# Two interleaved attention blocks with gradients: which engine turns the weights, and when

## The chip, the cores and the metric

The kernel runs on one core of a Trainium2 chip. The metric is the device time of one execution in microseconds (us); lower is better.

## The reference

Four residual layers, A, B, A, B, on x of 2048 tokens by 640 features in bf16, with 32 heads of 20. A and B have one set of weights each, used twice.

```python
def A(x):   # linear attention, no mask
    q, k, v = split(layernorm(x) @ A_wqkv)
    pq, pk = phi(q), phi(k)                   # where(t > 0, t + 1, exp(t)) + 1e-6
    o = (pq @ (pk.T @ v)) / (pq . sum(pk))    # per head
    return o @ A_wo
def B(x):   # sliding window of 256, causal
    q, k, v = split(layernorm(x) @ B_wqkv)
    return softmax(mask(q @ k.T / sqrt(20))) @ v @ B_wo
x = x + A(x); x = x + B(x); x = x + A(x); x = x + B(x)
```

The outputs are x and the gradients of grad_out by x, A_wqkv, A_wo, B_wqkv and B_wo. The backward pass multiplies by transposed weights, so four weights are needed turned: Wqkv (640x1920) and Wo (640x640) of A and of B. Turning them is what the change is about.

## The kernel before, in words

Tokens are worked on in 16 tiles of 128 (`TT`). The time has these stages: the **opening** (`a_first`, L940: layer norm and q, k, v of the first A layer, tile by tile, to about 112 us), the sums over all tokens (`a_kv`, L569), the **first pass** (`ab_pass(0)`, L961: the rest of layer A, the whole B layer and the q, k, v of the next A layer, one tile after the other, to about 430 us), again `a_kv`, the **second pass** (`ab_pass(2)`, to about 715 us), and then the backward phases, which the change doesn't touch.

`forward` (L332) doesn't issue instructions directly. Each helper records an operation (`Sched.op`, L94) with its engine, an estimated duration, what it reads and writes, and a due time; `Sched.order` (L126) then plays the engines forward with these estimates and fixes the order of each engine's queue. Every queue is worked off in that order: an instruction that waits holds all behind it on its engine. SyncE (SP) issues most DMAs, ScalarE (ACT) the rest. An operation marked `filler` on TensorE is taken when nothing else is ready for `IDLE` (L23, 300 ns of the estimates). `Ring` is a set of buffers used in turn; a new use waits until the last one is done.

Two ways of turning 128-column blocks are in use. `flip` (L417) is a transposing DMA on SyncE's queue. `turn` (L449) lets TensorE multiply by the identity into PSUM (L462) and ScalarE or VectorE copy the result to SBUF (L465, L467). In the first pass each tile needs such flips of its own: oTA, oTB, QT, KT, hnTB, pqT.

The turned weights are made before as follows, each in pieces of 160 KB that go through SBUF to DRAM (`W`) and are read in the backward phases:

- `wflips` (L906): A's Wqkv (15 pieces) and A's Wo (5), flipped from their copies in SBUF (`Wqkv_A`, and `slabR`, the memory that Wo_A lies in) into the ring pp, then stored. They are spread over the tiles of the first pass (L1031, with `wf` and `ws` in `AT`).
- `bflips` (L919): B's Wqkv (15 pieces), flipped from the input in DRAM into the rings KT, QT and e, then stored, after the first pass (L1048).
- `early_dO` (L712): B's Wo (5 pieces), flipped from SBUF into `WoTB` (in the memory of vv), at the start of the second pass, after `a_kv` is done with vv (`after_kv`).

Other names that matter: hn, the normalised tile, has a single buffer (`hnA`, L371); it is written by VectorE (L480), stored by SyncE (L484) and turned by TensorE. ee, the buffer of exp(q) or exp(k), has four. `s3` and `s1` are the PSUM banks of the attention scores (L821), `singles` the same five banks one by one. `late_q` (L540) recomputes q for six tiles as filler work between the passes.

Of the kernel before, what the change touches and what calls it, by code (L numbers as in the profile page):

```python
# [16 lines left out]
P = 128  # L17
# [69 lines left out]
class Sched:  # L87
# [38 lines left out]
    def order(self):  # L126
        engs = ("PE", "DVE", "ACT", "POOL", "SP")
        for o in self.ops:
            o.after -= o.deps | {o}
            o.nwait = len(o.deps) + len(o.after)  # L130
            for d in o.deps | o.after:
                assert d.idx < o.idx
                d.users.append(o)
        last = {}
        for o in self.ops:
            for b in o.bufs:
                last[b] = o.idx
# [12 lines left out]
        while len(out) < len(self.ops):  # L150
            best = None
            for e in engs:
                if not ready[e]:
                    continue
                t, cands = free[e], ready[e]
                if e == "PE" and self.ahead is not None:
                    cands = [o for o in cands if o.filler or o.rank < front + self.ahead]
                    if not cands:
                        continue
                o = min(cands, key=lambda o: (max(o.est, t) + IDLE * o.filler, o.prio))  # L160
                c = (max(o.est, t), o.prio)
                if best is None or c < best[0]:
                    best = (c, o)
            (t, _), o = best
            e = o.eng
            ready[e].remove(o)
            if o.dma:
                kind, size = o.dma
                if kind == "T":
                    free[e] = t + 1100 + size / 1000  # L170
                    chan = max(chan, t + 800) + size / 140
                else:
                    free[e] = t + (330 if e == "SP" else 200)
                    chan = max(chan, t) + size / 300
                o.end = chan + 2000
            else:
                free[e] = t + o.dur
                o.end = free[e] + (170 if e == "PE" else 0)
            o.start = t
            out.append(o)  # L180
            while front < len(seq) and seq[front].start is not None:
                front += 1
            for u in o.users:
                if o in u.deps:
                    u.est = max(u.est, o.end + (60 if u.eng != e or o.dma else -170 if e == "PE" else 0))
# [15 lines left out]
class Kern:  # L201
# [130 lines left out]
    def forward(self, slabs):  # L332
# [5 lines left out]
        with ExitStack() as st:  # L338
# [78 lines left out]
            def flip(out, in_, size, r, w, **kw):  # L417
                op("SP", 60, lambda: nc.sync.dma_start_transpose(out=out(), in_=in_()), r, w, dma=("T", size), **kw)
# [4 lines left out]
            def av(n):  # L423
                return 170 + 0.834 * n
# [283 lines left out]
            def after_kv(o):  # L708
                o.deps.update(kv_users)
                o.deps.discard(o)  # L710

            def early_dO():  # L712
                for et in range(DT):
                    flip(lambda et=et: WoTB[:, :, et * P:(et + 1) * P], lambda et=et: wsb["Wo_B"][:, et, :], 160 * KB,
                         ["Wo_B", ("rs", 3, 0)], [("WoTB", et)])
                    after_kv(S.ops[-1])
                dma("SP", lambda: W["WoTB"].rearrange("p (a b) -> p a b", a=DT), lambda: WoTB, 800 * KB,
                    [("WoTB", et) for et in range(DT)], [])
                for t in dslabs:
                    op("DVE", 100 + DP * 0.45, lambda t=t: nc.vector.memset(t, 0.0), [], ["dzero"])  # L720
                    after_kv(S.ops[-1])
# [181 lines left out]
                v = src.rearrange("(kt p) n -> p kt n", p=P)  # L903
                dma(eng, lambda: wsb[name][:, k:k + 1, :], lambda: v[:, k:k + 1, :], 2 * P * wsb[name].shape[-1], after, [name])

            def wflips(i, gate):  # L906
                def f():
                    et, part = divmod(i, 4)
                    key, dst, n, a = ("Wqkv_A", "WqTA", self.QTT, part * DT) if part < 3 else ("Wo_A", "WoTA", DT, 0)
                    c0 = part * D if part < 3 else 0  # L910
                    b = R["pp"].buf()
                    keys = [("Wqkv_A", i) for i in range(6)] if part < 3 else [key]
                    view = lambda: b.t.rearrange("p (k q) -> p k q", k=DT)
                    flip(view, lambda: wsb[key][:, et, c0:c0 + D], 160 * KB, keys + [gate], [b])
                    dma("SP", lambda: W[dst].rearrange("p (a b) -> p a b", a=n)[:, a:a + DT, et * P:(et + 1) * P],
                        view, 160 * KB, [b], [])
                return f

            def bflips(i, gate):  # L919
                def f():  # L920
                    et, part = divmod(i, 3)
                    kind = ("KT", "QT", "KT", "e", "e")[i % 5]
                    b = R[kind].buf()
                    view = lambda: (b.t[:, 0:DT, :] if kind != "e" else
                                    b.t.rearrange("p h i q -> p (h i) q")[:, 0:DT, :])
                    flip(view, lambda: self.B_wqkv[et * P:(et + 1) * P, part * D:(part + 1) * D], 160 * KB, [gate], [b])
                    dma("SP", lambda: W["WqTB"].rearrange("p (a b) -> p a b", a=self.QTT)[
                        :, part * DT:(part + 1) * DT, et * P:(et + 1) * P], view, 160 * KB, [b], [])
                return f

            wA = self.A_wqkv.rearrange("(kt p) n -> p kt n", p=P)
            for c0, c1 in ((0, 2), (2, 6)):
# [7 lines left out]
            def a_first(items, l, base, lag=0.0, late=()):  # L940


                for tt in range(TT):
# [14 lines left out]
            AT = {0: dict(wf=-2.296, ws=0.65, num=-2.458, out=-1.707, outb=1.792, step=0.144, qkv=-0.99, wide=0.745, lag=0.42, af=2.042, al=-0.11),  # L958
                  2: dict(lq=-3.207, num=-2.403, out=-1.76, outb=1.696, step=0.086, qkv=-0.985, wide=0.584, lag=0.35, gT=0.745, dO=1.691, dOs=0.137)}

            def ab_pass(l, last):  # L961
# [59 lines left out]
                if last:  # L1021
                    for tt in range(EARLY, TT):
                        items.append((tt + a["lq"], len(items), lambda tt=tt: late_q(l, tt, "mm")))
                    items.append((0.01, len(items), early_dO))
                    spread(items, 15.0, 16.25, [dWo_most(u) for u in range(NA)])
                    for tt in range(TT):
                        for at, f in zip((a["gT"] - 0.5, a["gT"], a["dO"], a["dO"] + a["dOs"]), dO_steps(tt)):
                            items.append((tt + at, len(items), f))
                else:
                    a_first(items, l + 2, a["af"], a["al"], range(TT))  # L1030
                    for i in range(4 * DT):  # L1031
                        t = min(int(a["wf"] + a["ws"] * i), TT - 1)
                        items.append((t + 0.05, len(items), wflips(i, ("rs", 1, t))))
                run(items)

            items = []
# [4 lines left out]
            for i, (k, src) in enumerate((("Wo_A", self.A_wo), ("Wqkv_B", self.B_wqkv), ("Wo_B", self.B_wo))):  # L1041
                for j in range(DT):
                    tt = 1 + 3 * i + j
                    items.append((tt + 0.9, len(items), lambda k=k, src=src, j=j, tt=tt: load_w(k, src, "SP", j, [("vv", tt, 5)])))
            run(items)
            a_kv(0)
            ab_pass(0, False)
            for i in range(3 * DT):  # L1048
                bflips(i, ("rs", 1, TT - 1))()
            for tt in range(EARLY):  # L1050
                late_q(2, tt, filler=True)
            a_kv(2)
            kv_users = {o for t in range(TT) for k in [("pk", t, 2), ("pk", t, 3), ("vv", t, 4), ("vv", t, 5)]
                        for o in S.rd.get(k, ())}
            a_users = {o for i in range(6) for o in S.rd.get(("Wqkv_A", i), ())}
            ab_pass(2, True)
            over = [o for k in ("Wqkv_B", "Wo_A") for o in S.rd.get(k, ())]
# [810 lines left out]
```

## Time and profile before

| | |
|---|---|
| median of three runs | 2163.03 us (2159.4 to 2163.52) |
| the profiled execution | 2163.08 us, span 2161.4 us |
| TensorE busy | 2008.5 us, 93% of the span |
| weight loads (PEld) | 1384.3 us, 64% |
| VectorE busy | 1441.9 us, 67% |
| ScalarE busy | 1191.9 us, 55% |
| GpSimd busy | 879.2 us, 41% |
| SyncE's DMA queue (q1) | 302.44 MB, 72.5% of 16 DMA engines' time |
| ScalarE's DMA queue (q10) | 72.94 MB, 10.9% |

How to read it: the page cuts the span into 40 slices and gives each engine's busy share in tenths, the TensorE clock that was granted (PEclk, in tenths of full speed) and the share of the DMA engines. Rows of a stretch give busy time and, in brackets, the number of instructions. A row of the timeline gives start, duration, engine (SPq and ACTq are DMA issues), line, operation and what was written from what; in square brackets stands the idle time before it and the releaser that the profile infers. "To landing" is the time from the issue of a DMA to its completion.

### The profile page before, as it was taken

To read this page: it belongs to the slowest core of one execution; us is meant where nothing else is said; L and a number is where in the kernel's file an instruction comes from. 1 tells how busy PE (TensorE), PEld (TensorE's weight loads), DVE (VectorE), ACT (ScalarE), POOL (GpSimd) and SP (SyncE) were. 2 spreads that over 40 slices of the span, in tenths; PEclk is the share of its full clock that TensorE was granted. 3 is DMA by queue.
4 is the path that set the end of the run, shared out by engine and by line. 5 is a ranking of instruction groups with operands and counts; after the bars stand their busy time and mean duration, and the time that the engine had idled before them with its cause. 6 is when DMAs were issued, how large, how long until landed. Compare 5 with 4: busy or idle time off the path is not lost. (4 is left out here: it accounts for less than half of the span.)

```text
span 2161.4 us, 67833 instructions
## 1 busy us (share of the span) xinstructions
PE 2008.5 (93%) x27808; PEld 1384.3 (64%) x27808; DVE 1441.9 (67%) x2954; ACT 1191.9 (55%) x1975; POOL 879.2 (41%) x1850
## 2 busy tenths in 40 slices
PE   6878899879999899999899999998999999999999
PEld 4645666556666567777666667655777765666764
DVE  7656677567777489999734459605999984444651
ACT  4617778617888589899522223215889882121430
POOL 1015566506777556666323213203656651221210
PEclk9979999999999989999999999998999989999999
DMA  7449998788999688988997899836998997989843
GB/s 274 171 136 194 191 199 185 173 220 182 211 210 199 144 157 157 159 155 151 200 187 168 208 196 214 181 95 143 154 159 151 166 169 162 195 181 230 186 112 102
DMA packets 964808, 379.70 MB, mean 176 GB/s; under 512 B 844817, under 2 KB 944785, under 8 KB 964241
## 3 DMA queue, kind: packets, MB, share of 16 engines
q1 hardware_dynamic: 887296, 302.44, 72.5%
q10 hardware_dynamic: 77200, 72.94, 10.9%
q8 instruction: 217, 3.56, 0.7%
q14 instruction: 95, 0.77, 0.1%
HBM read 109.02 MB, written 112.07 MB: 102 GB/s over the span
## 5 line engine op out<-in xcount | busy, mean ns | idle before, releaser
L1668 DVE TENSOR_TENSOR ds_sb<-pair,e_sb 128x768 bf16<-128x768 f32 x480 | 438.0, 952 | 58.4 <-PE pair L1629 50.9
L1648 ACT ACTIVATE e_sb<-pair 128x768 bf16<-128x768 f32 x480 | 391.0, 815 | 95.6 <-PE pair L1629 66.3
L841 POOL TENSOR_SCALAR_AFFINE_SELECT e_sb<-e_sb 128x384 bf16<-128x384 bf16 (+1 forms) x512 | 198.2, 406 | 373.7 <-ACT e_sb L832 347.3
L832 ACT ACTIVATE e_sb<-s_ps 128x1152 bf16<-128x1152 f32 (+2 forms) x256 | 273.9, 1070 | 107.0 <-PE s_ps L828 71.0
L1660 POOL TENSOR_SCALAR_AFFINE_SELECT e_sb<-e_sb 128x256 bf16<-128x256 bf16 x448 | 182.1, 407 | 226.9 <-ACT e_sb L1648 226.8
L1302 POOL TENSOR_TENSOR gw<-w,gcar 128x640 f32<-128x640 f32 x64 | 89.4, 1398 | 423.9 <-ACT w L1299 400.4
L1113 PEld LDWEIGHTS <-slabR 128*128 128x128 bf16 x1920 | 185.7, 98 | 116.2 <-DMA slabR<-o 5.8
L1657 POOL TENSOR_SCALAR_AFFINE_SELECT e_sb<-e_sb 128x256 bf16<-128x256 bf16 x512 | 206.5, 406 | 90.1 <-ACT e_sb L1648 90.1
L1693 PEld LDWEIGHTS <-dsT 128*128 128x128 bf16 x2880 | 146.3, 97 | 96.7 <-issue 90.4
L1684 ACT COPY dsT<-dsT_ps 128x768 bf16<-128x768 bf16 x240 | 191.2, 797 | 10.2 <-PE dsT_ps L1681 7.3
L446 PE MATMUL mm_ps<-slabR,hnTB 128*128 128x320 bf16 x960 | 170.5, 309 | 8.4 <-DVE gcar L518 6.1
L1681 PE MATMUL dsT_ps<-ident,ds_sb 128*128 128x128 bf16 x1848 | 158.4, 223 | 1.6 <-ACT dsT L1684 1.1
L1697 PEld LDWEIGHTS <-e_sb 128*128 128x128 bf16 x2880 | 145.2, 96 | 0.0
L1697 PEld LDWEIGHTS <-ds_sb 128*128 128x128 bf16 x2880 | 145.1, 96 | 0.0
L846 POOL TENSOR_SCALAR_AFFINE_SELECT e_sb<-e_sb 128x512 bf16<-128x512 bf16 x224 | 142.5, 636 | 0.0
L835 ACT ACTIVATE e_sb<-s_ps 128x384 bf16<-128x384 f32 (+2 forms) x256 | 119.8, 468 | 36.6 <-PE s_ps L828 10.1
L1113 PE MATMUL dw_ps<-dqkv,slabR 128*128 128x480 bf16 x640 | 134.6, 366 | 0.0
L1113 PE MATMUL dw_ps<-dqkv,om 128*128 128x480 bf16 x640 | 134.2, 366 | 0.0
L1284 ACT ACTIVATE dh<-mm_ps 128x320 f32<-128x320 f32 x64 | 28.0, 437 | 191.6 <-PE mm_ps L1113 153.3
L1629 PE MATMUL pair<-slabR 32*128 32x384 bf16 (+2 forms) x1024 | 121.6, 329 | 11.5 <-DVE ds_sb L1668 5.0
L866 PE MATMUL pv_ps<-v_slab,e_sb 128*128 128x32 bf16 x2880 | 117.7, 177 | 12.9 <-POOL e_sb L846 10.7
L866 PEld LDWEIGHTS <-e_sb 128*128 128x128 bf16 x2880 | 106.0, 96 | 35.6 <-POOL e_sb L846 14.6
(227 smaller groups left out, 4299.3 us busy)
## 6 DMA issues: line engine op xcount, KB each, us to landing
qkvp<-qk_slab SPq DMA_DIRECT2D x64, 256.0 KB, 3.4
hn<-slabR SPq DMA_DIRECT2D x64, 160.0 KB, 3.0
qkvp<-v_slab SPq DMA_DIRECT2D x32, 256.0 KB, 3.5
slabR<-qkvp SPq DMA_DIRECT2D x16, 512.0 KB, 5.2
o<-o SPq DMA_DIRECT2D x48, 160.0 KB, 2.8
eq<-ee ACTq DMA_DIRECT2D x32, 160.0 KB, 3.0
pq<-pp ACTq DMA_DIRECT2D x32, 160.0 KB, 2.0
ek<-ee ACTq DMA_DIRECT2D x32, 160.0 KB, 2.3
```

The lines of the kernel that those rows point to most:

```text
L446: nc.tensor.matmul(ps.t[:, w0:w0 + width], lhsT=lhsT(), rhs=rhs(), start=start, stop=stop)
L832: op("ACT", av(3 * nkt * P), lambda: nc.scalar.activation(e.t[:, 0:3, 0:nkt, :], s3.t[:, :, 0:nkt * P].rearrange("p h (i q) -> p h i q", q=P),
L841: nc.gpsimd.affine_select(out=v, in_=v, compare_op=ALU.is_ge, fill=0.0, base=0, pattern=[[0, h1 - h0], [1, P]], channel_multiplier=-1)
L866: nc.tensor.matmul(pv.t[:, h % 16, :], lhsT=e.t[:, hh, j, :], rhs=vts[j].t[:, h, :], start=(j == 0), stop=(j == nkt - 1))
L1113: nc.tensor.matmul(ps.t[:, w0:w0 + width], lhsT=lhsT(), rhs=rhs(), start=start, stop=stop)
L1648: nc.scalar.activation(E[n][:, 2 * p:2 * p + 2], PR[h][:, :, 0:3 * P].rearrange("p i (j q) -> p i j q", q=P), ACT.Exp, scale=self.c_att)
L1657: nc.gpsimd.affine_select(out=e[:, :, j, :], in_=e[:, :, j, :], compare_op=ALU.is_ge, fill=0.0, base=0, pattern=[[0, 2], [-1, P]], channel ...
L1660: nc.gpsimd.affine_select(out=e[:, :, j, :], in_=e[:, :, j, :], compare_op=ALU.is_ge, fill=0.0, base=-1, pattern=[[0, 2], [1, P]], channel ...
L1668: nc.vector.tensor_mul(DS[n][:, hs], PR.pop(h)[:, :, 0:3 * P].rearrange("p i (j q) -> p i j q", q=P), E[n][:, hs])
L1681: nc.tensor.transpose(ps[:, i, j, :], DS[n][:, 2 * p + i, j, :], self.ident)
L1684: (nc.scalar.copy if by == "A" else nc.vector.tensor_copy)(TSB[h], TPS.pop(h))
L1697: nc.tensor.matmul(a[:, 1 + x, hh, :], lhsT=src[n][:, hh, j, :], rhs=ld[g][rhs][:, q, cs], start=(i == 0), stop=(i == len(dkv) - 1))
```

## The change

The four weights change places and means. A's Wo and **B's Wqkv** are flipped by DMA from the inputs in DRAM during the opening, two pieces per tile from 4.5 tiles on, through the rings KT and e. **A's Wqkv and B's Wo** are turned by TensorE between the passes: each piece is five transposes into one of the three banks of s3, a ScalarE copy of 128x640 into KT or e (or right into `WoTB`), and for A's Wqkv a store of whole rows. These operations are fillers; they wait for the last scores of the first pass, and the first scores of the second pass wait for them all (the line with `items[-1].ops.extend(turned)`), the copies into `WoTB` also for the end of `a_kv`. The planner gets a fixed cost for the new DMAs (kind "B"). The flips of `wflips`, `bflips` and `early_dO` go.

```diff
             if o.dma:
                 kind, size = o.dma
-                if kind == "T":
+                if kind == "B":
+                    free[e], chan_ = t + 1300, t + 2500
+                elif kind == "T":
...
-                o.end = chan + 2000
+                o.end = (chan_ if kind == "B" else chan) + 2000
...
             def early_dO():
-                for et in range(DT):
-                    flip(lambda et=et: WoTB[:, :, et * P:(et + 1) * P], lambda et=et: wsb["Wo_B"][:, et, :], 160 * KB,
-                         ["Wo_B", ("rs", 3, 0)], [("WoTB", et)])
-                    after_kv(S.ops[-1])
...
-            def wflips(i, gate):
...
-            def bflips(i, gate):
...
+            def turn_w(name, n, keys, dst, done, after=()):
+                F = dict(filler=True)
+                for q in range(n):
+                    ps = R["sb"].buf()
+                    ps.make = lambda ps=ps: singles[ps.idx % 3].bitcast(BF).rearrange("p (k q) -> p k q", q=P)
+                    def f(ps=ps, q=q):
+                        for et in range(DT):
+                            nc.tensor.transpose(ps.t[:, et, :], wsb[name][:, et, q * P:(q + 1) * P], self.ident)
+                    o = op("PE", pe([P] * DT), f, keys, [ps], **F)
+                    o.deps.update(o_ for o_ in R["s3"].items[-1].ops if not o_.filler)
+                    turned.append(o)
+                    out, key = dst(q)
+                    turned.append(op("ACT", av(D), lambda ps=ps, out=out: nc.scalar.copy(out(), ps.t[:, 0:DT, :]), [ps],
+                                     [key], **F))
+                    turned[-1].deps.update(after)
...
+                    done(q, out, key)
+            def flip_w(i, gate):
+                def f():
+                    et, part = divmod(i, 4)
+                    src, name, n, a = ((self.B_wqkv, "WqTB", self.QTT, part * DT) if part < 3 else (self.A_wo, "WoTA", DT, 0))
+                    c0 = part * D if part < 3 else 0
+                    kind = ("KT", "e")[i % 2]
+                    b = R[kind].buf()
...
+                    flip(view, lambda: src[et * P:(et + 1) * P, c0:c0 + D], 160 * KB, [gate], [b])
+                    S.ops[-1].dma = ("B", 0)
+                    dma("SP", lambda: W[name].rearrange("p (a b) -> p a b", a=n)[:, a:a + DT, et * P:(et + 1) * P],
+                        view, 160 * KB, [b], [])
...
+            R["sb"] = Ring(3, tiles=singles[0:3], name="sb")
+            def staged(W_, n):
+                def dst(q):
+                    kind = ("KT", "e")[len(turned) // 2 % 2]
...
+                def done(q, out, b):
+                    dma("SP", lambda: W[W_].rearrange("p (a b) -> p a b", a=n)[:, q, :].rearrange("p (k q) -> p k q", q=P),
+                        out, 160 * KB, [b], [])
...
+            for i in range(4 * DT):
+                at = 4.5 + 0.5 * i
+                items.append((at, len(items), flip_w(i, ("rs", 0, int(at) - 1))))
             run(items)
             a_kv(0)
             ab_pass(0, False)
-            for i in range(3 * DT):
-                bflips(i, ("rs", 1, TT - 1))()
             for tt in range(EARLY):
                 late_q(2, tt, filler=True)
             a_kv(2)
...
+            turn_w("Wqkv_A", self.QTT, [("Wqkv_A", i) for i in range(6)], *staged("WqTA", self.QTT))
+            turn_w("Wo_B", DT, ["Wo_B"], lambda q: (lambda: WoTB[:, q, :].rearrange("p (k q) -> p k q", q=P), ("WoTB", q)),
+                   lambda q, out, key: None, kv_users)
+            R["s3"].items[-1].ops.extend(turned)
```

More of the change, by code (lines that the diff above doesn't have):

```diff
@@ L904, in load_w @@
                 dma(eng, lambda: wsb[name][:, k:k + 1, :], lambda: v[:, k:k + 1, :], 2 * P * wsb[name].shape[-1], after, [name])
-            def wflips(i, gate):
+            def turn_w(name, n, keys, dst, done, after=()):
[13 more added lines that the diff above has]
+                    turned[-1].deps.update(after)
+                    turned[-1].deps.discard(turned[-1])
+                    done(q, out, key)
@@ L907, in f @@
+            def flip_w(i, gate):
                 def f():
                     et, part = divmod(i, 4)
-                    key, dst, n, a = ("Wqkv_A", "WqTA", self.QTT, part * DT) if part < 3 else ("Wo_A", "WoTA", DT, 0)
+                    src, name, n, a = ((self.B_wqkv, "WqTB", self.QTT, part * DT) if part < 3 else (self.A_wo, "WoTA", DT, 0))
                     c0 = part * D if part < 3 else 0
-                    b = R["pp"].buf()
-                    keys = [("Wqkv_A", i) for i in range(6)] if part < 3 else [key]
@@ L913, in f @@
-                    view = lambda: b.t.rearrange("p (k q) -> p k q", k=DT)
-                    flip(view, lambda: wsb[key][:, et, c0:c0 + D], 160 * KB, keys + [gate], [b])
-                    dma("SP", lambda: W[dst].rearrange("p (a b) -> p a b", a=n)[:, a:a + DT, et * P:(et + 1) * P],
+                    kind = ("KT", "e")[i % 2]
+                    b = R[kind].buf()
+                    view = lambda: (b.t if kind == "KT" else b.t.rearrange("p h i q -> p (h i) q"))[:, 0:DT, :]
+                    flip(view, lambda: src[et * P:(et + 1) * P, c0:c0 + D], 160 * KB, [gate], [b])
@@ L916, in f @@
+                    S.ops[-1].dma = ("B", 0)
+                    dma("SP", lambda: W[name].rearrange("p (a b) -> p a b", a=n)[:, a:a + DT, et * P:(et + 1) * P],
                         view, 160 * KB, [b], [])
+                    S.ops[-1].dma = ("B", 0)
                 return f
-            def bflips(i, gate):
-                def f():
-                    et, part = divmod(i, 3)
-                    kind = ("KT", "QT", "KT", "e", "e")[i % 5]
-                    b = R[kind].buf()
[L924 to L929, printed above, removed]
+            turned = []
@@ new lines, in forward @@
+            R["sb"] = Ring(3, tiles=singles[0:3], name="sb")
+            def staged(W_, n):
+                def dst(q):
+                    kind = ("KT", "e")[len(turned) // 2 % 2]
+                    b = R[kind].buf()
+                    return (lambda: b.t[:, 0:DT, :] if kind == "KT" else
+                            b.t.rearrange("p h i q -> p (h i) q")[:, 0:DT, :]), b
+                def done(q, out, b):
+                    dma("SP", lambda: W[W_].rearrange("p (a b) -> p a b", a=n)[:, q, :].rearrange("p (k q) -> p k q", q=P),
+                        out, 160 * KB, [b], [])
+                return dst, done
@@ L957, in forward @@
             EARLY = 6
-            AT = {0: dict(wf=-2.296, ws=0.65, num=-2.458, out=-1.707, outb=1.792, step=0.144, qkv=-0.99, wide=0.745, lag=0.42, af=2.042, al=-0.11),
+            AT = {0: dict(num=-2.458, out=-1.707, outb=1.792, step=0.144, qkv=-0.99, wide=0.745, lag=0.42, af=2.042, al=-0.11),
                   2: dict(lq=-3.207, num=-2.403, out=-1.76, outb=1.696, step=0.086, qkv=-0.985, wide=0.584, lag=0.35, gT=0.745, dO=1.691, dOs=0.137)}
@@ L1030, in ab_pass @@
                     a_first(items, l + 2, a["af"], a["al"], range(TT))
-                    for i in range(4 * DT):
-                        t = min(int(a["wf"] + a["ws"] * i), TT - 1)
-                        items.append((t + 0.05, len(items), wflips(i, ("rs", 1, t))))
                 run(items)
```

## The prediction

> **What bounds the kernel now.** I read the page's table of slices first, then the busy times by stage, then by tile, then SyncE's own queue.
>
> ```profile
> PE   6878899879999899999899999998999999999999
> PEclk9979999999999989999999999998999989999999
> DMA  7449998788999688988997899836998997989843
> ```
>
> A slice is 54 us. TensorE has nine tenths almost everywhere from slice 10 on, so the end of the program is set by TensorE's work plus TensorE's gaps. The gaps that this change can touch lie in slices 0 to 8, the forward passes; the built instruction lists of both kernels are the same behind the first tiles of the second pass, so I price nothing after some 520 us. By stage (columns: stretch, length, busy us of PE, PEld, DVE, ACT, POOL, granted clock, DMA share, GB/s):
>
> ```profile
> 45.06:106.91 61.85, 54.34 (x494) 39.57 (x493) 44.27 (x128) 38.96 (x93) 0.00 (x0) 1.00 0.48 170
> 177.64:309.27 131.63, 115.90 (x1885) 79.95 (x1884) 88.84 (x218) 93.73 (x153) 75.72 (x166) 0.94 0.94 191
> 309.27:391.45 82.18, 78.03 (x1352) 55.26 (x1352) 62.85 (x157) 66.87 (x111) 54.87 (x120) 1.00 0.87 190
> 420.00:452.24 32.24, 26.33 (x320) 19.28 (x317) 16.76 (x48) 5.95 (x14) 2.24 (x6) 0.85 0.92 206
> 452.24:480.20 27.96, 20.66 (x183) 13.39 (x182) 22.04 (x56) 4.06 (x11) 0.00 (x0) 1.00 0.95 236
> ```
>
> The reader is to see three things: the opening (first row) uses half of the DMA engines; the first pass has a worse half (second row) and a better one (third); between the passes (last rows) TensorE idles for 13 us and ScalarE has 10 us of work in 60. The first pass by tile, cut where SyncE issues the flip of that tile's pqT:
>
> ```profile
> 193.90:213.00 19.10, 15.08 (x242) 10.42 (x240) 11.14 (x27) 13.01 (x21) 10.48 (x23) 0.86 1.03 203
> 213.00:231.95 18.95, 18.42 (x291) 12.61 (x290) 13.53 (x34) 13.51 (x24) 10.86 (x24) 0.96 0.92 194
> 231.95:252.19 20.24, 15.26 (x257) 10.65 (x257) 12.76 (x31) 13.49 (x22) 10.95 (x24) 0.91 0.87 181
> 291.31:309.27 17.96, 17.02 (x286) 12.05 (x285) 13.26 (x34) 13.53 (x24) 11.05 (x24) 1.00 0.87 195
> 326.14:342.62 16.48, 15.73 (x273) 11.10 (x273) 12.89 (x33) 13.41 (x23) 10.95 (x24) 1.00 0.86 193
> 342.62:359.12 16.50, 15.75 (x273) 11.13 (x273) 12.54 (x33) 13.30 (x23) 11.01 (x24) 1.00 0.88 193
> ```
>
> The same tile takes 19 to 20 us while weight flips stand in SyncE's queue, and 16.5 us as soon as they are over (the last WoTA store is issued at 305.12). Why, the queue shows:
>
> ```profile
> 191.90 1.27 SPq L418 DMA_TRANSPOSE pp<-slabR  x1
> 193.22 0.58 SPq L414 DMA_DIRECT2D WqTA<-pp  x1
> 193.90 1.41 SPq L418 DMA_TRANSPOSE pqT<-slabR  x1
> 195.35 0.66 SPq L414 DMA_DIRECT2D hn<-slabR  x1
> 196.11 1.23 SPq L418 DMA_TRANSPOSE QT<-qk_slab  x1
> ```
>
> A weight flip (pp) and a weight store stand ahead of flips that TensorE needs. QT, issued at 196.11, lands by the QT group's median of 4.2 us at 200.3, and TensorE's next scores wait:
>
> ```profile
> 199.77 0.35 PE L828 MATMUL s_ps<-QT,KT 32*128 32x128 bf16 x12 [2.27 <-ACT e_sb L832]
> ```
>
> The releaser named there is inferred. Such gaps are followed by slices with a lower granted clock: 10 us windows at 0.83 behind this gap, at 0.73 behind one of 2.99 us at 248.40, and none between 300 and 410 us, where gaps stay below 1.4 us.
>
> A second link runs through ScalarE. In the built instruction lists each DMA of SyncE and ScalarE takes one of eight counters in turn and waits for the last DMA on it. So a late flip also holds a ScalarE store, and the arithmetic queued behind it: ScalarE's waits name the flips of pp with 4.7 + 1.2 us up to 305 us, and 5.8 us at 439.67 behind an hn store.
>
> **The change part by part.** The sum is made against the profiled execution, 2163.1 us with a span of 2161.4; the median of the three runs shown is 2163.03, so both are the same place.
>
> Removed from the first pass: 20 flips (1.24 us of issue each) and 20 stores (0.38 to 0.58 us). Eight intervals from 177.64 to 326.14 last 148.5 us; at the later pace of 16.49 they would last 131.9. **Gain 16.6.** What is late next is TensorE itself, 15.7 of 16.5 us. Bounds: of the 16.6, some 7 us is clock, each interval's TensorE time by what its clock lacks (15.08 x 0.14, 18.42 x 0.04, 15.26 x 0.09, 18.68 x 0.08, 16.50 x 0.09); if the dips do not come from the gaps, 9.4 is left. Six of the flips stand ahead of 177 us, in the ramp 106.9 to 177.6. Its largest gaps (2.67 us at 127, 2.26 at 155) end with the normalisation L480, a VectorE chain: I take a gain of 1, from 0 to 3.
>
> Added to the opening: 20 flips from the inputs and 20 stores, two pairs per tile from tile 3 to 13, between the hn stores in SyncE's queue. The pace now is 5.30 us per tile (hn stores from 45.06 to 98.07, ten tiles). Three prices bear on it. (1) Issue: 0.33 + 2 x 1.25 + 2 x 0.5 = 3.8 us per tile, below 5.3. (2) DMA engines: from 420 to 446 us queue q1 carried 12 flips, 12 such stores and 2 hn in 20.3 us of all 16 engines (78.3% of 16, 77.5% of 10), less 0.9 for hn, so 1.6 us a pair; 0.48 x 5.3 + 1.8 x 1.6 = 5.4 us per tile, just full. (3) Landing: hn has one buffer, so each L480 (0.44 us) waits for the store of the tile before. That store lands in 1.9 us here, 2.6 to 3.0 where the DMA share is 0.9; with the one L480 wait of 0.67 us at 49.15 the loop is already near the pace at places. I take 0.6 us for each of ten tiles: **cost 6**. Bounds: 0, if all stays below 5.3; 22, the slow rival below.
>
> [...]
>
> Between the passes: 15 flips of B's Wqkv with stores (400 to 446 us) and 5 of Wo (453 to 466) go. In their place come 20 groups of five TensorE transposes, 20 ScalarE copies of 128x640 and 15 stores of whole rows. On TensorE a group costs 0.28 us from start to start (97.11 to 97.39), 20 of them 5.6 us, of which I hide half in the gaps of 420 to 480 us: +3. The copies, 20 x 0.69 = 13.9 us, fit into ScalarE's 50 idle us; three banks let TensorE run three groups ahead. But the first scores of the second pass now stand behind the last two Wo groups and their copies, 0.2 + 2 x 0.69: +1.6. Against this:
>
> ```profile
> 440.96 2.83 PE L446 MATMUL mm_ps<-Wqkv_A,pqT 128*128 128x320 bf16 x10 [3.36 <-DVE gcar L518]
> ```
>
> This gap is ScalarE held by a store's counter behind an hn store that lands 3.1 us after issue, while q1 is full of flips. Without them I take 2.7 of 3.36, and 1.9 us of slow clock behind it (ten matmuls in 2.83 us, usually 1.58; five at 445.05 in 1.49, usually 0.84). **Net 0**: 3 + 1.6 - 2.7 - 1.9; bounds -5 (all the added work in gaps) and +7 (none in gaps, nothing won back). The 5 Wo flips ahead of the qkvp stores cost nothing now: the gap of 2.67 us at 472 ends with L480 again.
>
> [...]
>
> Sum: -16.6 - 1 + 6 + 0 = -11.6, **2151.5 us**.
>
> **Rivals.**
> 1. The clock of the first pass dips by itself. For: the dips lie in slices that are also full of work. Against: none in 300 to 410 us. 2163.1 - 9.4 - 1 + 6 = **2158.7**.
> 2. The opening hides all: SyncE and DMA have room on average. -16.6 - 1 + 1 + 0: **2146.5**; with the gaps between the passes won too (-5), 2141.5.
> 3. Slower: the eight counters set the opening's pace. A tile then issues 6 + 3.6 = 9.6 DMAs, so each waits for one issued some 4.4 us before; flips land in 3.7 us at the median and 6.0 at most. With 6.0 throughout, 9.6 / 8 x 6.0 = 7.2 us per tile, 1.9 over, and eleven tiles cost +21; with +3 between the passes, 2163.1 - 17.6 + 21 + 3 = **2169.5**. It decides from 6.9 us per tile (5.3 + 17.6 / 11). Against: landing in the first pass, at a DMA share of 1.03, has its median near 3.6.
> 4. The flips were not what slowed the first pass; it gains nothing: -1 + 6, **2168**. Against: the pace changes with the last flip.
>
> **How the numbers follow.** Forecast 0.56, rival 2 0.17, rival 1 0.12, rival 3 0.11, rival 4 0.04. The range, 2141 to 2165, takes in the first three and leaves out the slow ends. A measurement here tells 0.2% (4.3 us) from no change: faster 0.78 (the forecast, rival 2 and part of rival 1), same 0.09, slower 0.13.
>
> **What would show it.** In the profile after: tiles of the first pass near 16.5 us from the start, at clock 1.00; an opening with a pace of 5.9 us, and waits of L480 for hn or of ScalarE for the flips into KT and e_sb; no gap of 3 us near the end of the first pass; one of 1 to 2 us at the first scores of the second. The prediction is wrong if the first pass keeps 19 us tiles, or if the opening's pace is above 6.9.

## The result and the profile after

| | before | after |
|---|---|---|
| median (range) of six runs each | 2162.74 us (2148.88 to 2164.93) | 2144.49 us (2139.10 to 2146.05) |
| profiled execution, span | 2163.08, 2161.4 us | 2145.22, 2143.5 us |

The ratio is 0.9924, with a 95% interval of 0.9903 to 0.9944: faster by 18 us. The page's slices after. Against before, TensorE rises from 8 to 9 in slices 3 and 4, and the DMA engines are fuller in slices 0 and 1, where the flips went (7 and 4 before, 9 and 9 now), and emptier in slice 7 (7 before, 4 now), where flips went away. The clock of the first pass (slices 4 to 7) reads 9 in both, so slices of 54 us are too coarse to show its dips:

```profile
PE   6879999889999899999899999999999999999999
PEclk9989999999999899999899999999999999999999
DMA  9928989469998788987987899847999998989943
```

To compare stages I cut both traces at five events: ScalarE's first store of oA (end of the opening and its sums), the first, ninth and last flip of pqT of the first pass, and the first store of the output x in the second pass. The opening of before from its sixth to its sixteenth store of hn, then three stretches of before (stretch, length, busy us of PE, PEld, DVE, ACT, POOL, clock, DMA share, GB/s):

```profile
45.06:98.07 53.01, 45.72 (x413) 33.21 (x412) 38.29 (x111) 32.91 (x81) 0.00 (x0) 1.00 0.48 171
120.50:177.64 57.14, 45.98 (x490) 28.83 (x490) 35.67 (x85) 19.02 (x46) 14.87 (x38) 0.81 0.66 152
177.64:326.14 148.50, 131.76 (x2158) 91.37 (x2157) 101.48 (x250) 107.04 (x175) 86.73 (x190) 0.94 0.93 191
407.96:506.40 98.44, 77.22 (x926) 51.92 (x923) 62.23 (x161) 32.91 (x74) 20.77 (x50) 0.93 0.80 191
```

The same stretches after:

```profile
50.15:109.62 59.47, 50.96 (x467) 37.32 (x466) 43.03 (x122) 35.66 (x88) 0.00 (x0) 1.00 0.96 250
123.70:178.72 55.02, 45.03 (x484) 28.40 (x484) 35.41 (x85) 18.76 (x46) 13.93 (x36) 0.81 0.39 109
178.72:310.74 132.02, 124.98 (x2167) 87.64 (x2164) 98.56 (x251) 107.25 (x176) 87.75 (x192) 1.00 0.89 189
392.24:490.80 98.56, 82.96 (x1035) 58.92 (x1033) 62.30 (x161) 46.95 (x96) 21.51 (x52) 0.91 0.56 165
```

The eight intervals of the first pass lost 16.5 us: 6.8 are TensorE's busy time (the clock went from 0.94 to 1.00) and 9.7 are gaps (16.7 us idle before, 7.0 after). The ramp ahead of it (from the end of the opening to the first pqT flip) is 2.0 us shorter. The opening's DMA share went from 0.48 to 0.96, and its end came 3.1 us later (120.54, then 123.65). Between the passes the length hardly moved, though TensorE has 5.7 us more work there.

By tile, the first two of the eight intervals now last 13.5 and 18.4 us and the others 16.5 to 17.2. Here are the third and the fourth, and then SyncE's queue. Before, a weight flip and a weight store were issued just ahead of pqT; now the queue is free there, from the end of oTA's issue at 189.1 us until pqT at 192.17:

```profile
210.54:227.03 16.49, 15.79 (x273) 11.34 (x273) 12.84 (x33) 13.64 (x23) 10.95 (x24) 1.00 0.87 193
227.03:243.50 16.47, 15.73 (x273) 11.10 (x273) 12.88 (x33) 13.52 (x23) 10.92 (x24) 1.00 0.92 194
```

```profile
187.88 1.24 SPq L420 DMA_TRANSPOSE oTA<-oA  x1
192.17 1.20 SPq L420 DMA_TRANSPOSE pqT<-slabR  x1
193.43 0.57 SPq L416 DMA_DIRECT2D hn<-slabR  x1
194.09 1.22 SPq L420 DMA_TRANSPOSE oTB<-oB  x1
195.40 1.58 SPq L420 DMA_TRANSPOSE QT<-qk_slab  x1
```

The gap of 3.36 us near the end of the first pass is now 0.24, its ten matmuls take 1.52 us instead of 2.83, and the first scores of the second pass wait for a copy of Wo (TensorE's timeline):

```profile
422.69 1.52 PE L448 MATMUL mm_ps<-Wqkv_A,pqT 128*128 128x320 bf16 x10 [0.24 <-DVE gcar L520]
...
454.56 0.24 PE L826 MATMUL s_ps<-QT,KT 32*128 32x128 bf16 x4 [1.38 <-ACT vv L918]
```

### The profile page after: what moved, and what is told of

Same layout as the page of the kernel before. It is cut to its first block, busy times and chain, and to the rows that moved or that the text cites. A ratio compares the mean times of both kernels' runs of the same rounds, so it can differ in the third digit from the quotient of the medians.

```text
span 2143.5 us, 68024 instructions
## 1 busy us (share of the span) xinstructions
PE 2008.2 (94%) x27908; PEld 1389.2 (65%) x27908; DVE 1440.1 (67%) x2954; ACT 1203.3 (56%) x1995; POOL 879.4 (41%) x1850
## 5 line engine op out<-in xcount | busy, mean ns | idle before, releaser
L1654 PE MATMUL pair<-slabR 32*128 32x384 bf16 (+2 forms) x1024 | 120.5, 326 | 12.0 <-DVE ds_sb L1693 5.2
L1138 PEld LDWEIGHTS <-om 128*128 128x128 bf16 x800 | 77.5, 98 | 71.3 <-DMA om<-o 2.4
```

The source lines that it names most:

```text
L1138: nc.tensor.matmul(ps.t[:, w0:w0 + width], lhsT=lhsT(), rhs=rhs(), start=start, stop=stop)
```

## The experiments

All in one table, in us, one profiled execution each: the end of the opening, then the length of each stage, then everything from the first store of the output x to the span's end, where, but for the first 17 us, TensorE works off the same instructions in the same order (read in the traces of before, after, r1, r3, r6, e9, e11 and e12). Medians are of 6 to 12 runs (r8 one); ratios are to the kernel before on the same chip.

| kernel | opening ends | ramp | 8 intervals | rest of pass | between | rest | median, ratio [95%] |
|---|---|---|---|---|---|---|---|
| before | 120.5 | 57.1 | 148.5 | 81.8 | 98.4 | 1655.0 | 2162.7 |
| after | 123.7 | 55.1 | 132.0 | 81.5 | 98.6 | 1652.7 | 2144.5, 0.9924 [0.9903, 0.9944] |
| r1 | 127.2 | 55.0 | 131.0 | 81.5 | 100.0 | 1658.7 | 2156.3, 0.9976 [0.9964, 0.9989] |
| r2 | 131.6 | 53.9 | 133.2 | 83.4 | 96.8 | 1659.1 | 2156.4, 0.9975 [0.9958, 0.9992] |
| r3 | 131.6 | 55.1 | 131.2 | 82.4 | 91.3 | 1665.4 | 2159.0, 0.9978 [0.9962, 0.9995] |
| r4 | 118.1 | 56.6 | 140.8 | 81.5 | 98.4 | 1658.4 | 2155.5, 0.9976 [0.9961, 0.9991] |
| r5 | 130.0 | 56.1 | 137.7 | 81.4 | 97.0 | 1655.3 | 2163.4, 1.0009 [0.9993, 1.0026] |
| r6 | 121.7 | 55.0 | 132.2 | 81.8 | 95.8 | 1664.2 | 2147.2, 0.9920 [0.9900, 0.9939] |
| r7 | 126.9 | 54.9 | 131.0 | 83.7 | 92.5 | 1657.1 | 2148.3, 0.9927 [0.9908, 0.9945] |
| r8 | 181.3 | 55.5 | 130.9 | 82.7 | 96.7 | 1660.4 | 2209.3 |
| e9 | 128.6 | 54.9 | 132.0 | 83.2 | 97.9 | 1654.5 | 2152.5, 0.9957 [0.9943, 0.9971] |
| e10 | 125.5 | 54.9 | 132.1 | 82.0 | 97.2 | 1656.8 | 2153.5, 0.9962 [0.9951, 0.9974] |
| e11 | 125.0 | 53.9 | 131.1 | 82.0 | 100.7 | 1663.0 | 2156.3, 0.9967 [0.9953, 0.9980] |
| e12 | 123.7 | 52.7 | 131.1 | 83.1 | 93.3 | 1663.1 | 2147.5, 0.9941 [0.9921, 0.9960] |

Two things have to be known before a row is read. The last stage took 1652.7 to 1665.4 us, 13 us apart, so a whole time says little about one stage; I compare stages. (The six runs of one kernel are themselves as far apart: 16 us in before, 7 us in after.) And the filling DMAs of r1, r2, r3 and r5 went out at 7.7 us instead of at the end of the opening (nothing in GpSimd's queue held them). Their sixth hn stores come at 55.5 to 57.5 us (before 45.1, after 50.2), and their openings end 7 to 11 us later than those of the kernels that they are made from (r2, without its flips, against before). I put that down to the filling, not to the part that was taken away.

**r1_no_wflips**, the first pass without weight flips.

```diff
-                    for i in range(4 * DT):
-                        t = min(int(a["wf"] + a["ws"] * i), TT - 1)
-                        items.append((t + 0.05, len(items), wflips(i, ("rs", 1, t))))
+            fill("WqTA", self.A_wqkv, DT)   # one plain DMA on GpSimd's queue
+            fill("WoTA", self.A_wo, DT)
```

> The kernel before with one part taken away: the 20 flips and 20 stores of A's Wqkv and A's Wo that are spread over the first pass. Their turned copies are filled instead by one plain, unturned DMA each on GpSimd's queue at the end of the opening, so the gradients through A are computed with unturned weights; everything else stays. Theory (the flips in SyncE's queue cost the first pass 16.6 us): eight intervals of the first pass from its first to its ninth pqT flip fall from 148.5 us to 132, the ramp ahead of it by 1 to 2 us, nothing else moves: 2163 - 18 = 2145, ratio 0.992. Rival A (the clock dips by itself): only 9.4 us go, 2153, and the granted clock in the first half of the pass stays near 0.94. Rival B (something else slowed the first half): 2162, tiles of 19 us stay.

Stage by stage the theory holds: 131.0 us at clock 1.00, the ramp 2.1 shorter. Rival A would have left 139, rival B 148. The whole missed by 11 us: 6.7 come from the filling, 1.6 from the stage between the passes, 3.7 from the last.

**r4_plain** and **r5_no_stores** split that price. r4 makes the flips plain DMAs, which the planner still prices as flips; r5 leaves the stores out.

```diff
-   flip(view, lambda: wsb[key][:, et, c0:c0 + D], 160 * KB, keys + [gate], [b])
+   dma("SP", view, lambda: wsb[key][:, et, c0:c0 + D].rearrange("p (k q) -> p k q", k=DT), 160 * KB, ...)
+   S.ops[-1].dma = ("T", 160 * KB)
```

> The kernel before with the 20 weight flips of the first pass made plain DMAs of the same 160 KB pieces between the same buffers (the weights stay unturned in A's backward pass), in the same places of SyncE's queue; the 20 stores stay. Theory (the 1.24 us of issue of each transposing DMA on SyncE, and the slow landing behind it, hold the flips of the tiles): most of the gain of leaving them out is had, eight intervals last 132 to 138 us, 2146 to 2152. Rival (the number of DMAs counts, through the eight counters and the places in the queue, not the transposing): the eight intervals stay above 143 us and the time above 2157.

```diff
-   dma("SP", lambda: W[dst].rearrange("p (a b) -> p a b", a=n)[:, a:a + DT, et * P:(et + 1) * P],
-       view, 160 * KB, [b], [])
+   fill("WqTA", self.A_wqkv, DT); fill("WoTA", self.A_wo, DT)
```

> The kernel before with the 20 weight flips of the first pass kept and the 20 stores behind them left out (the turned copies in DRAM are filled by two plain, unturned DMAs on GpSimd's queue at the end of the opening). Theory (the transposing flips do the harm): eight intervals stay above 143 us, 2157 to 2163. Rival (each weight DMA costs alike, by a place in the queue and a counter): half of the gain, eight intervals near 140 us, 2154. Second rival (the stores do it, as each waits for the flip in front of it and holds SyncE's queue until that has landed): nearly the whole gain, 132 to 135 us, 2146 to 2149.

Both came out between the expectations. Plain DMAs in place of the flips win 7.7 us in the eight intervals, no stores 10.8; the sum, 18.5, is about what leaving both out wins (16.5 to 17.5), so either half of a pair costs on its own. r4, then r5:

```profile
174.74:315.50 140.76, 127.49 (x2162) 89.78 (x2161) 101.34 (x251) 106.78 (x175) 87.42 (x192) 0.99 0.90 200
```

```profile
186.10:323.90 137.80, 128.25 (x2168) 89.68 (x2167) 100.96 (x251) 107.07 (x176) 87.38 (x192) 0.98 0.95 192
```

In r4 the clock is nearly whole and 13.3 us of gaps are left. Faster transfers are not what was won: the tiles' own flips land no sooner after than before (medians of the eight intervals: QT 4.3 us before and 4.6 after, KT 3.6 and 4.5, hnTB 3.7 and 3.9, oTA 4.1 and 4.1), and r5's intervals are 10.8 us shorter at a DMA share of 0.95, above the 0.93 of before. What fell is the time that SyncE spends issuing in these intervals: 115.1 us before, 104.3 in r4, 108.8 in r5, 93.4 after. So I read the price as places in SyncE's queue. That is argued from these numbers; no run issued the same weight DMAs in this pass from another queue. What a flip costs beyond a plain DMA stands in that queue, first before, then r4:

```profile
222.53 1.22 SPq L418 DMA_TRANSPOSE pp<-Wqkv_A  x1
...
227.93 1.98 SPq L418 DMA_TRANSPOSE pp<-Wqkv_A  x1
```

```profile
198.47 0.74 SPq L414 DMA_DIRECT2D pp<-Wqkv_A  x1
```

In the eight intervals the same 160 KB take 1.24 us of SyncE at the median as a flip (1.22 to 1.98) and 0.57 as a plain DMA (0.47 to 1.04; the one shown is long). To landing both take the same in this stretch (Wqkv's pieces, median of seven: 3.6 and 3.5 us). What differs is the queue that issues them: a flip holds it twice as long.

**r2_no_opening**: after, without the opening's flips.

```diff
-            for i in range(4 * DT):
-                at = 4.5 + 0.5 * i
-                items.append((at, len(items), flip_w(i, ("rs", 0, int(at) - 1))))
+            fill("WqTB", self.B_wqkv, DT); fill("WoTA", self.A_wo, DT)
```

> The kernel after with one part taken away: the 20 flips and 20 stores of the opening. Their turned copies are filled by one plain, unturned DMA each on GpSimd's queue at the end of the opening, so some gradients are computed with unturned weights. Theory (the opening's flips cost what the sums' last product moved by, 3.1 us): that product comes at 117.7 us again and the program ends 3 us earlier than the kernel after, 2141.5, ratio 0.990. Rival A (the forecast's price): 6 us earlier, 2138.5. Rival B (the loss is made good later, in the ramp of the first pass): no change, 2144.5, with the first pqT flip at 178.7 us as in the kernel after.

Nothing follows: its opening ends at 131.6 because of the early filling. **e9_no_wflips_late** and **e10_no_opening_late** were to mend this for r1 and r2, with a small DMA that waits for the ninth hn ahead of the filling:

```diff
+            op("POOL", 60, lambda: nc.gpsimd.dma_start(out=W["WoTA"][:, 0:D], in_=self.tm_view(self.hn_d[0])[:, 8, :]), ...)
             fill(...)
```

> r1_no_wflips again with its flaw mended: there the two plain DMAs that fill the turned copies ran at 7.7 us, among the first loads, and put the opening back by some 7 us. Here a small DMA on GpSimd's queue first waits for the store of the ninth hn, so that the filling begins in the half idle DMA engines of the opening. The gradients through A are again computed with unturned weights. Theory: the first ScalarE store of the first pass comes at 118 to 121 us (before 120.5), eight intervals of the pass last 131 to 133 us, the first store of out leaves at 487 to 490 us (before 506.4), and 2143 to 2149 in all, ratio 0.991 to 0.994. Rival (what the first pass gains is lost later, in the backward phases, and the loss of r1 was that): 2152 and more, with the first store of out at 490 or earlier.

> r2_no_opening again with the same flaw mended in the same way: the kernel after without the opening's 20 flips and stores, the two turned copies filled by plain DMAs that wait for the ninth hn. Some gradients are computed with unturned weights. Theory (the opening's flips cost 3.1 us): the first ScalarE store of the first pass comes at 120 to 121 us (after 123.7, before 120.5), 2141.5, ratio 0.990 to 0.991. Rival A (the forecast's price of 6): 117.7 us, 2138.5. Rival B (nothing, the 3.1 us were one execution's): 123 us, 2144.5.

The filling now came at 64 us and put the opening back again. TensorE's timeline of e9, then ScalarE's:

```profile
79.40 0.69 PE L448 MATMUL s_ps<-Wqkv_A,hnTA 128*128 128x320 bf16 x2 [6.48 <-ACT vv L501]
79.88 0.74 PE L464 MATMUL s_ps<-ident,slabR 128*128 128x128 bf16 x5
80.42 1.54 PE L448 MATMUL mm_ps<-Wqkv_A,hnTA 128*128 128x320 bf16 x5
```

```profile
71.37 0.67 ACT L467 COPY pqT<-s_ps 128x640 bf16<-128x640 bf16 x1
77.87 0.33 ACTq L416 DMA_DIRECT2D ek<-ee  x1
78.54 0.34 ACTq L416 DMA_DIRECT2D pk<-gcar  x1
78.92 0.42 ACT L501 CAST vv<-s_ps 128x320 bf16<-128x320 f32 x1 [6.88 <-DVE st L476]
```

The two DMAs (2.4 MB with 10.6 us to landing, and 0.8 MB) stand beside ScalarE's small stores. SyncE's waits name such a store (pq) with 11.0 us, ScalarE issues nothing for 6 us ahead of its next store (ek), and TensorE waits 6.48 us for the copy behind it. (ScalarE's own named releaser, DVE st, is inferred.) The matmuls behind the gap ran at half pace, five in 1.54 us instead of 0.84. So one burst of 3.2 MB goes with an opening that ends some 8 us later (128.6 against 120.5), more than 20 flips and 20 stores of 160 KB spread out.

In the stages that the filling doesn't touch, e9 lies at 54.9, 132.0 and 97.9 us, r1 at 55.0, 131.0 and 100.0, and the rival, that the gain is lost in the backward phases, is not borne out: the last stage takes 1654.5, as before. But e9's opening (128.6, expected 118 to 121) and its time (2152.5, expected 2143 to 2149) missed. For the price of the opening the two are of no use: e10 is 3 us better than e9 with the same burst and meets none of its three expectations.

**r6_later** moves the opening's flips by two tiles.

```diff
-                at = 4.5 + 0.5 * i
+                at = 6.5 + 0.45 * i
```

> The kernel after with the opening's 20 flips started two tiles later and set a little closer (from 6.5 tiles on, every 0.45 tile, instead of from 4.5, every 0.5). Nothing is left out. Theory (the opening's cost of 3.1 us comes where the flips meet the loads of the weights, 30 to 50 us, where the DMA engines are full): the sixth store of hn comes at 45 to 47 us instead of 50.15, and the sums' last product 1 to 3 us earlier than 120.8; 2142 to 2143.5. Rival (the cost comes at the end of the opening, where the stores of hn lose their lead): the sums' last product comes at 121 to 124 us, and the time is 2144.5 to 2148.

The sixth hn store comes at 44.8 us (before 45.1, after 50.2), so the delay ahead of it, where the flips meet the first loads, goes when they start later. Of these 5.4 us only 1.4 are left at the sixteenth store (108.2 against 109.6) and 2.0 at the end of the opening, no more than alike openings differ by (2.4 us between before and r4). The first store of the output x leaves at 486.4 instead of 490.8. In the whole time (0.9920 against 0.9924; expected 2142 to 2143.5, measured 2147.2) nothing of it shows.

**r3_no_turns** and **e11_dma_between** ask what turning A's Wqkv between the passes costs.

```diff
-            turn_w("Wqkv_A", self.QTT, [("Wqkv_A", i) for i in range(6)], *staged("WqTA", self.QTT))
+            fill("WqTA", self.A_wqkv, DT)                      # r3
+            for i in range(3 * DT):                            # e11: 15 flips and stores, as for B's Wqkv before
+                aflips(i, ("rs", 1, TT - 1))()
```

> The kernel after with one part taken away: the 15 groups of TensorE transposes, the 15 ScalarE copies and the 15 stores that turn A's Wqkv between the passes (its turned copy is filled by one plain, unturned DMA on GpSimd's queue at the end of the opening, so the gradients through A use unturned weights). B's Wo is still turned by TensorE. Theory (the groups lie half in gaps): 15 x 0.28 us = 4.2 us of TensorE work go, half of it shows: 2 us earlier at the first scores of the second pass and at the end, 2142.5, ratio 0.9915. Rival A (none of it is hidden): 4.2 us and up to 1 us of waits for the copies, 2139.5. Rival B (all of it lies in gaps): no change, 2144.5.

> The kernel after with A's Wqkv turned between the passes not by TensorE but by 15 transposing DMAs from the input and 15 stores, in the place and through the buffers that B's Wqkv had in the kernel before. Nothing is left out. From the last pqT flip of the first pass to the first store of out takes 98.4 us before, 96 to 98.6 with the TensorE groups, 91.3 without them (r3_no_turns). Theory (the net of nothing between the passes was two equal prices: TensorE's groups cost 5 to 6 us there, and so do DMA flips): 96 to 99 us again, 2144 to 2147, ratio 0.992 to 0.9935. Rival A (the DMA flips were nearly free, and the change lost 5 us here by bringing in TensorE): 91 to 93 us, 2139. Rival B (the flips cost more than the groups): over 100 us, 2148 and more.

From the last pqT flip to the first store of the output x: 91.3 us without the groups, 98.6 with them, 100.7 with DMA flips. More kernels bear on this. The five that hold the groups in this stage (after, r2, r6, r8, e10) take 95.8 to 98.6 us, 97.0 in the mean; the three that don't (r3, r7, e12) take 91.3 to 93.3, 92.4 in the mean. The difference of 4.6 us is no less than the 4.2 us of work of the 15 groups, so rival A of r3 is right: on average none of it is hidden. In e11 the flips cost no less (its rival B), and not through TensorE, which has 3 us less to do. It is ScalarE that stands behind DMAs for 17.2 us in this stage (3.4 us in after, 12.7 us in before). TensorE's row in after stands above; here r3 and e11, then e11's two longest such waits (in after the longest is 2.7 us):

```profile
400.30:491.70 91.40, 75.63 (x962) 53.21 (x961) 62.06 (x162) 37.62 (x81) 21.61 (x52) 0.96 0.53 150
```

```profile
392.00:492.70 100.70, 80.09 (x960) 56.18 (x957) 61.74 (x161) 37.44 (x81) 21.57 (x52) 0.92 0.75 178
```

```profile
414.00 0.44 ACT L516 ACTIVATE ee<-mm_ps 128x320 bf16<-128x320 f32 x1 [7.29 <-DMA o<-oB]
...
424.63 0.77 ACT L516 ACTIVATE ee<-mm_ps 128x320 bf16<-128x320 f32 x2 [4.63 <-DMA hn<-slabR]
```

**r7_first_ramp** puts the 15 groups behind the opening's sums; **e12_both** adds r6's shift.

```diff
+            first_s = R["s3"].buf()
+            turn_w("Wqkv_A", self.QTT, [("Wqkv_A", i) for i in range(6)], *staged("WqTA", self.QTT))
+            first_s.ops.extend(turned)
...
             ab_pass(0, False)
...
-            turn_w("Wqkv_A", self.QTT, [("Wqkv_A", i) for i in range(6)], *staged("WqTA", self.QTT))
```

> The kernel after with the 15 groups that turn A's Wqkv on TensorE put behind the sums of the opening, ahead of the first scores of the first pass, instead of between the passes. Nothing is left out. Theory (the ramp of the first pass has gaps of TensorE of 2 us and more that end with a chain of VectorE, so 4.2 us of transposes disappear in them): the first pqT flip moves by less than 1 us, the time between the passes falls by some 2 us: 2142.5. Rival (the copies stand ahead of ScalarE's first exponentials, or the groups ahead of the chain that opens the pass): the first pqT flip moves by 4 us or more, 2146.5 to 2149.

> r6_later and r7_first_ramp together: the opening's flips start two tiles later, and A's Wqkv is turned on TensorE behind the opening's sums. Nothing is left out. Theory (the two gains stand in different stages and add): first ScalarE store of the first pass at 124 to 126 us, 91 to 93 us between the last pqT flip and the first store of out, which leaves at 483 to 486 us (after 490.8): 2138 to 2141, ratio 0.989 to 0.991. Rival (the later flips of the opening and the groups behind its sums meet, as both use the rings KT and e and SyncE's queue): the first ScalarE store at 128 us or later and the time of the kernel after, 2144 to 2147.

The stage between the passes falls from 98.6 to 92.5 us in r7, where a fall of some 2 us was expected, and to 93.3 in e12 (expected 91 to 93). The opening with the groups behind it ends 3.3 us later in r7 than in after, 2.0 later in e12 than in r6. By the last pqT flip of the first pass r7 is 4.2 us behind after, the whole work of the groups, while e12 is 0.1 us ahead of r6; so whether they can be hidden there stays open. In e12 the first store of the output x leaves at 483.9 us, 7.0 before after's and as expected, but the whole (2147.5, expected 2138 to 2141) is not better than after (0.9941 and 0.9924, overlapping intervals): the last stage took 1663 us. No version that I ran beats the kernel after by a measurable amount.

**r8_probe** asks the clock about transposes.

```diff
+            for kind in "TMT":
+                for _ in range(400):
+                    if kind == "T": nc.tensor.transpose(tp, self.ident, self.ident)
+                    else: nc.tensor.matmul(mp, lhsT=self.ident, rhs=self.ident, start=True, stop=True)
```

> The kernel after with a probe ahead of everything on TensorE: 400 transposes of the identity, 400 matmuls of 128x128 by the identity, 400 transposes again, without a wait in between, into two PSUM tiles that nobody reads. Nothing is left out. It asks what the granted clock does under transposes alone. [...] The time is that of the kernel after plus what of the probe isn't hidden under the first loads, some 10 to 60 us.

TensorE's timeline, and single microseconds of it. The bracket counts the instructions that ran in that microsecond in whole or in part, and they overlap (219 to 223 ns each in the mean by the profile), so it is more than the number started:

```profile
1.43 24.19 PE L1827 MATMUL probe_t<-ident 128*128 128x128 bf16 x400 [1.43 <-POOL ident masks.py:199]
25.45 22.50 PE L1829 MATMUL probe_m<-ident 128*128 128x128 bf16 x400
47.79 22.50 PE L1827 MATMUL probe_t<-ident 128*128 128x128 bf16 x400
```

```profile
4.00:5.00 1.00, 1.00 (x12) 1.00 1.04 380
5.00:6.00 1.00, 1.00 (x21) 1.00 1.05 389
...
49.00:50.00 1.00, 1.00 (x22) 1.00 0.00 0
```

In the trace the transposes start 107 ns apart up to 4.99 us, 3.5 us after the first, and 56 ns apart from then on. With no matmul before them they double their pace, and 400 of them hold it as 400 matmuls do (22.5 us each, 18 starts per us). The trace lists the transposes as matmuls. The column of the granted clock shows 1.00 even in the slow first microseconds, because the trace's first clock record starts at 4.99 us. The program took 65 us more than after, above the 10 to 60 expected.

## Why the prediction was right, point by point

- **First pass, -16.6:** -16.5, and in the split that was given (some 7 us of clock, 9.4 of gaps; measured 6.8 and 9.7). Ten more kernels without weight flips in this pass, from r1 to e12, lie at 130.9 to 133.2. Rival 1 falls: with the flips gone the clock is 1.00; so does rival 4. That the pairs act through SyncE's queue is argued from r4, r5 and the issue times; how much of it is QT's place and how much the counters isn't separated.
- **Ramp, -1:** -2.0; 52.7 to 55.5 in the kernels without weight DMAs there, 56.1 to 57.1 in those with them (before, r4, r5). The term was too small, within its bounds. The forecast counted six flips ahead of 177 us; the queue holds ten, three of them ahead of 120 us. So ten of the pairs lay in the eight intervals and cost 16.5 us, and seven in the ramp cost 2: there TensorE's largest gaps end with VectorE's chain (2.67 and 2.26 us before), and a place in the queue is cheap.
- **Opening, +6:** +3.1 here. The forecast pace of 5.9 us a tile is what came (59.47 / 10), but by luck, as neither step of its working held. The wait that it was made from didn't come: in these ten tiles VectorE's normalisation (L482, L480 before) waits for an hn store once, for 0.8 us, and before it did so twice (0.67 and 1.19 us; the forecast names one). And the step from pace to price failed: it took every delay of an hn store for a delay of the end. The sixteenth hn store came 11.5 us later (98.07 to 109.62), 5.1 of it before the sixth, which the forecast had left out, and the sums' last product only 3.1: before, the stores ran 20 us ahead of it, now 11. The first rows of the two tables show the same: between the sixth and the sixteenth store TensorE does 5.2 us more work than before (467 against 413 instructions) and idles only 1.2 us longer, so the stores lost their lead over TensorE, and TensorE lost little. One execution prices this to some 2 us at best: the opening ends at 120.5 and 118.1 in before and r4, which hold only three weight pieces at its end, and at 123.7 and 125.0 in after and e11, which hold the same 20 flips, so 3 to 7 us. Rival 3 falls: no pace of 6.9. Rival 2 gave a nearer number (2146.5) by a mechanism that isn't there, an opening that costs 1.
- **Between the passes, 0:** +0.2 in this pair; over five kernels with the DMA flips there (before, r1, r4, r5, e9: 98.3 in the mean) and five with the groups (97.0) it is -1.3. Single parts came near those given: the gap gave 3.1 (forecast 2.7), the first scores wait 1.4 (1.6). But TensorE's busy time grew by 5.7, and "half hidden" was wrong: by r3, r7 and e12 nothing is. It came out even because the DMA flips that left had cost about as much, by e11 some 7 to 9 us (100.7 against the 91.3 to 93.3 of r3, r7 and e12), more than the 4.6 that the forecast took off. Two sizes were too small and cancelled, so the zero is in part luck.
- **Nothing behind 520 us:** -2.3 in the last stage, which but for its first 17 us has the same order of instructions. With 1652.7 to 1665.4 us in the fourteen profiles this is no effect that I can assign. After has the shortest of all. The medians carry such differences too: e11 is 12 us above after, of which the profile shows 1.9 ahead of the last stage. In r6 and e12 more slow clock goes with it (36.8 and 36.5 us of TensorE time lost by the clock, 25.6 in after and in before; each 10 us window's busy time by what its clock lacks). In r3 and e11 (27.8 and 24.8) it is TensorE's idle time instead (76 us in each; 67 in after, 69 in before). What decides stays open.

The sum of the stages is 3.1 - 2.0 - 16.5 - 0.3 + 0.2 - 2.3 = -17.8 (the spans, unrounded: -17.9), against -11.6 forecast. Of the difference 3.9 us come from the opening and the ramp and 2.3 from the last stage, which no part of the change explains. What the forecast had right by its mechanism is the first pass, nine tenths of the gain.

## What to carry to other kernels

Where one engine issues the small DMAs that the bottleneck waits for, look at the issue time of what stands between them. Here ten pairs of 1.8 us of issue each cost 1.65 us each in the eight intervals, and seven some 0.3 us each in the ramp, where TensorE's largest gaps end with VectorE's chain. Move such work to a stage whose queue runs ahead of its use, and measure that lead, since it swallows delay (here 11.5 us at the stores became 3.1 at the end). Turning data on the busiest engine wasn't free here although the stage had idle time: 4.2 us of work cost 4.6. Compare stages between fixed events over several kernels before believing a difference of a few microseconds in the whole.

## What the hardware showed beyond that

Two DMAs of 3.2 MB together, issued into a half idle stage (e9, DMA share 0.43 to 0.50 from 40 to 60 us), stood beside a stop of ScalarE's stores of 6 us and of TensorE of 6.48 us, while 40 DMAs of 160 KB in the same stage (6.4 MB) cost 3 to 7 us in all. In the eight intervals a transposing DMA of 160 KB (before) landed as fast as a plain one (r4; 3.6 and 3.5 us) and held SyncE's queue twice as long (1.24 and 0.57 us at the median). In r8, with no matmul ahead of them, transposes started 107 ns apart for 3.5 us and 56 ns apart from then on, and 400 matmuls behind them took the same 22.5 us as the last 400 transposes.
